# Attention in 64x64 quadrants with all steps placed anew, and MoE2 rows split one by one at unit 0

## The chip, the cores and the metric

The kernel runs on one core of one Trainium2 chip. The metric is the device time in microseconds of one execution; it is the median of the timed runs. A profile is one more execution, taken with the hardware profiler, and it has a time of its own.

## What is computed

Three stages follow one another on 4608 tokens of 512 numbers, all f32.

```python
kv  = einsum('bhsd,bhse->bhde', k, v)         # 8 batches, 8 heads, 576 tokens, 64 wide
out = einsum('bhsd,bhde->bhse', q, kv)
x   = out / sqrt(mean(out*out, -1) + 1e-6) * g_norm     # rows of 8 heads x 64
# MoE 1: 8 experts, the two best of noisy logits, 512 -> 1024 -> 512
nl  = x @ w_gate + log1p(exp(x @ w_noise)) * noise
x   = sum over the two: weight * relu(x @ w1[e]) @ w2[e]
# MoE 2: only rows with x @ w_skip > 0, the best of 8 experts, result added to x
x   = x + gate * relu(x @ w21[e]) @ w22[e]
```

## The kernel before

**Attention** (lines 300 to 870) runs over four pairs of batches. A batch is loaded as 128 partitions x 4 tokens (512 tokens, `load_kv`, `load_q`), and the remaining 64 tokens of two batches together as 128 partitions (`load_rest`). `kv_half` (L414, L419) sums k-transposed times v of four heads: 128x128 matmuls of two tokens each, of which the diagonal 64x64 blocks are wanted. Two copies and an addition (L422, L424, L313) bring the sums into a block-diagonal tile `kvbd` of 160 columns per head: 2 x 64 of kv and 2 x 16 of the router's gate columns, which `gate_columns` makes from kv (L440 to L449). The output runs in 56 steps (`subs`), 14 for each pair: transpose q of two or three heads on TensorE (`q_transposed`, L461) two steps ahead, copy (L464 or L466), multiply with `kvbd` (`out_sub`, L479; L485 and L486 for the remaining tokens), copy out (L488 or L490), square (L493 or L495), sum (L499). `finish` then makes the inverse root mean square of up to 16 values a row (L515 to L519, and a Newton step in `log_recip_newton`, L144 to L146), scales the rows on GpSimd (L523), sums the logits (L544, L547) and splits the rows into two f16 halves (L527 on ScalarE, L530 on VectorE), which SP writes to `xrows` in DRAM (L705, L709).

The order of all this is written by hand. Each step has three slots, and `at(step, f, slot)` puts a call there; the constants at the head of the file say where (`KV`, `GC`, `FIN`, `ROUTE`, `WSTEPS`, `EPLAN`, `CLEAR`) and which engine copies or squares (`QTE`, `OSBE`, `SQE`). All engines and SP's DMA queue run in the order of the program.

**Routing** (`route_half`) ranks the tokens of four batches in 27 pieces; the first half is placed by `ROUTE` beside the steps of the later pairs, the second runs in the **tail**: `TAIL` lists the order of its pieces ("r"), of what is left of `finish` ("f") and of the pieces of four early tiles of expert 0 ("0" to "3", `early_tile`, L734 to L753). Then the loop over the experts of MoE 1 begins with a gather of rows and a transposing DMA (L1055, L1057).

**MoE 2** works in units of one or two tiles of 128 rows of one expert (`moe2_unit`). `layer1` makes four pieces (for two tiles) and calls `point(p)` after each; ScalarE and VectorE make the two f16 halves of the hidden rows (L238, L239); `layer2` follows (L269). The rows of the next units are gathered in `later`, squared (`row_scales`, L931) at point 1 and split (`split_parts`, L938, L939) at point 3, in both cases all rows of a unit at once, and transposed by SP (L1194). The weights of a later unit are gathered behind the last tile of a unit (`rank_weights`, L1147), 2 MB each for `wa` and `wb`.

## Time and profile before

| | us |
|---|---|
| timed runs | 1273.98, 1275.65, 1279.09 |
| median | 1275.65 |
| profiled execution | 1287.97 |
| its span, first to last instruction | 1285.8 |

Busy shares of the profiled span: TensorE 92%, VectorE 64%, ScalarE 52%, GpSimd 29%. Times in the rows are counted from the span's start. A busy TensorE is not TensorE at its peak, since its ends are modelled; the pitch from start to start tells the price of a matmul in a row of them. "issue" is time in which an engine waited for nothing that the profile shows.

### The profile page before, as it was taken

To read this page: it belongs to the slowest core of one execution; us is meant where nothing else is said; L and a number is where in the kernel's file an instruction comes from. 1 tells how busy PE (TensorE), PEld (TensorE's weight loads), DVE (VectorE), ACT (ScalarE), POOL (GpSimd) and SP (SyncE) were. 2 spreads that over 40 slices of the span, in tenths; PEclk is the share of its full clock that TensorE was granted. 3 is DMA by queue.
4 is the path that set the end of the run, shared out by engine and by line. 5 is a ranking of instruction groups with operands and counts; after the bars stand their busy time and mean duration, and the time that the engine had idled before them with its cause. 6 is when DMAs were issued, how large, how long until landed. Compare 5 with 4: busy or idle time off the path is not lost.

```text
span 1285.8 us, 25287 instructions
## 1 busy us (share of the span) xinstructions
PE 1187.7 (92%) x9341; PEld 843.1 (66%) x9341; DVE 822.6 (64%) x3014; ACT 663.4 (52%) x1209; POOL 372.7 (29%) x454
## 2 busy tenths in 40 slices
PE   5868779999999999999999999999899999899996
PEld 5767667666666666676767576676666666576664
DVE  1667887535686777687677878778877665232231
ACT  2578663156564765675666767557664331132110
POOL 2223242211323232323333233232332331312220
PEclk8979789999999999999999999999999999999998
DMA  9999984748996978699698899989995673866570
GB/s 238 277 248 298 320 222 102 183 141 265 276 239 173 242 252 230 189 241 291 145 301 275 240 326 253 282 226 252 317 291 179 165 206 114 255 218 209 181 246 16
DMA packets 311410, 293.33 MB, mean 228 GB/s; under 512 B 205023, under 2 KB 256223, under 8 KB 307181
## 3 DMA queue, kind: packets, MB, share of 16 engines
q1 hardware_dynamic: 288316, 208.22, 61.8%
q0 software_dynamic: 22384, 82.36, 18.4%
q8 instruction: 75, 1.23, 0.4%
q10 hardware_dynamic: 576, 1.05, 0.2%
q14 instruction: 59, 0.48, 0.1%
HBM read 172.86 MB, written 93.42 MB: 207 GB/s over the span
## 4 chain that ended last, share of the span: by engine, by line
PE 52%; issue 15%; DVE 13%; ACT 11%; POOL 3%; another core or an unknown queue 2%; SPq 2%; DMA 1%; POOLq 0%; DVEq 0%; ACTq 0%
PE b L269 24%; PE a L230 21%; ACT wa L188 2%; PE kvps L414 1%; ACT hh L238 1%; DVE xh L939 1%; DVE x L1113 1%; ACT wb L188 1%; POOL out_dram L1211 1%; PE b L479 1%; PE small L968 1%; ACT ysb L1109 1%; DVE hl L239 1%; ACT presplit L188 1%
## 5 line engine op out<-in xcount | busy, mean ns | idle before, releaser
L230 PEld LDWEIGHTS <-wa 128*128 128x128 f16 x5184 | 460.0, 99 | 68.3 <-issue 21.3
L230 PE MATMUL a<-xT,wa 128*128 128x256 f16 (+6 forms) x3648 | 389.9, 267 | 8.3 <-issue 5.5
L269 PE MATMUL b<-wb,hh 128*128 128x512 f16 x1488 | 339.8, 379 | 8.7 <-ACT hh L238 8.5
L269 PEld LDWEIGHTS <-hh 128*128 128x128 f16 x1488 | 140.2, 98 | 170.8 <-ACT hh L238 19.5
L238 ACT ACTIVATE hh<-a 128x512 f16<-128x512 f32 (+5 forms) x186 | 107.1, 578 | 223.0 <-PE a L230 187.1
L239 DVE SCALAR_TENSOR_TENSOR hl<-a,hh 128x512 f16<-128x512 f32 (+5 forms) x186 | 125.1, 675 | 99.8 <-ACT hh L238 91.6
L269 PE MATMUL b<-wb,hl 128*128 128x512 f16 x744 | 175.8, 379 | 0.0
L1055 POOL DMA_INDIRECT xg<-xrows,idxp x67 | 65.6, 979 | 327.4 <-DVE orow L1079 287.0
L269 PEld LDWEIGHTS <-hl 128*128 128x128 f16 x744 | 72.2, 98 | 88.4 <-DVE hl L239 3.0
L230 PE MATMUL a<-x2Tr,wa 128*128 128x256 f16 (+1 forms) x1152 | 110.2, 258 | 8.1 <-DMA x2Tr<-xh 7.6
L1109 ACT ACTIVATE ysb<-b,gate 128x512 f32<-128x512 f32 x73 | 49.8, 682 | 128.3 <-PE b L269 68.8
L1117 POOL DMA_INDIRECT out_dram<-x,oi x67 | 68.3, 1020 | 137.2 <-DVE pi L1025 62.9
L171 ACT ACTIVATE wjunk<-stage 128x1024 bf16<-128x1024 f32 x96 | 101.3, 1055 | 2.1
L189 DVE SCALAR_TENSOR_TENSOR presplit<-stage,wscl,presplit 128x1024 f16<-128x1024 f32 x64 | 80.5, 1279 | 16.1 <-ACT presplit L188 16.1
L1088 POOL DMA_INDIRECT yo<-ydram,gi x67 | 70.9, 1059 | 51.1 <-issue 17.7
L188 ACT ACTIVATE presplit<-stage,wscl 128x1024 f16<-128x1024 f32 x64 | 71.3, 1141 | 17.9 <-DVE wscl L181 16.5
L479 PE MATMUL b<-kvbd,qTs 128*128 128x160 f32 x256 | 52.8, 346 | 21.9 <-issue 10.0
L931 ACT ACTIVATE jk<-x 128x512 bf16<-128x512 f32 x67 | 42.3, 631 | 54.6 <-DVE x L1113 48.3
L938 ACT ACTIVATE xh<-x,x2ss 128x512 f16<-128x512 f32 x67 | 45.4, 715 | 33.1 <-DVE x2ss L137 29.9
L523 POOL TENSOR_TENSOR osb<-osb,rinv 128x1024 f32<-128x1024 f32 (+1 forms) x20 | 37.1, 1854 | 87.0 <-DVE rinv L146 71.3
L479 PEld LDWEIGHTS b<-kvbd,qTs 128*128 128x128 f32 x256 | 42.6, 219 | 26.6 <-issue 10.9
L1113 DVE TENSOR_TENSOR x<-ysb,yo 128x512 f32<-128x512 f32 x67 | 46.4, 692 | 18.5 <-ACT ysb L1109 14.7
(356 smaller groups left out, 1529.8 us busy)
## 6 DMA issues: line engine op xcount, KB each, us to landing
stage<-in_moe_w_dram SPq DMA_DIRECT2D x32, 2048.0 KB
wsd<-presplit SPq DMA_DIRECT2D x8, 2056.0 KB
ydram<-ysb SPq DMA_DIRECT2D x64, 256.0 KB
wsd<-presplit SPq DMA_DIRECT2D x8, 2048.0 KB
out_dram<-zeros SPq DMA_DIRECT2D x9, 1024.0 KB
km<-in_k_dram SPq DMA_DIRECT2D x16, 512.0 KB
vm<-in_v_dram SPq DMA_DIRECT2D x16, 512.0 KB
qm<-in_q_dram SPq DMA_DIRECT2D x16, 512.0 KB
```

What stands on the lines that cost most here:

```text
L171: A.activation(junk, st[:, F * c:F * c + F], AF.Square, accum_out=acc[:, c:c + 1], **kw)
L188: A.activation(hi[:, d], st[:, d], AF.Copy, scale=sc)
L189: V.scalar_tensor_tensor(lo[:, d], st[:, d], sc, hi[:, d], op0=ALU.mult, op1=ALU.subtract)
L230: PE.matmul(ps[:, i, :], a[:, c, fs], xT[:, b + c, 0:nt], start=(n == 0), stop=(n == 11))
L238: behind[0] = A.activation(hh[:, fsl, 0:nt], ps, AF.Relu).ins
L239: i = V.scalar_tensor_tensor(hl[:, fsl, 0:nt], ps, 0.0, hh[:, fsl, 0:nt], op0=ALU.max, op1=ALU.subtract)
L269: PE.matmul(ps, a[:, f, gsl], b[:, f, :], start=(fs.start == 0 and i == 0), stop=(fs.stop == 8 and a is hl and f == 7))
L479: PE.matmul(po[:, i, :], qT[:, i, :], kvb[b % 4][:, h0 + i, :], start=True, stop=True)
L1055: G.indirect_dma_start(out=xg[:, g], out_offset=None, in_=xrows, in_offset=bass.IndirectOffsetOnAxis(ap=idx[:, t0 + g:t0 + g + 1], axis=0))
L1088: G.indirect_dma_start(out=yo, out_offset=None, in_=ydram[0:BASE[e], :], in_offset=bass.IndirectOffsetOnAxis(ap=gi[:, g:g + 1], axis=0), b ...
L1109: A.activation(ysb, ps, AF.Copy, scale=gate[:, g:g + 1])
L1117: s = G.indirect_dma_start(out=out, out_offset=bass.IndirectOffsetOnAxis(ap=oi[:, g:g + 1], axis=0), in_=x2[:, g], in_offset=None, bounds_ ...
```

## The change

**Loads.** q, k and v of four heads of a batch are loaded as 64 partitions x 9 tokens, the even heads on the lower 64 partitions and the odd heads on the upper ones; nine tokens of a head are one piece of 2304 bytes. There is no rest to load. Noise and router columns (`aux`) follow the same layout.

**Products.** kv of a pair of batches is summed in 64x64 quadrants: the row half `c` is the parity of the head, the column half `bl` the batch of the pair. `kv_out` copies the sums into `kvb` (two tiles in place of four, 80 columns per head and batch, no zeros) and GpSimd copies each half onto the other partitions. The output has 40 steps, ten for each pair: four heads of both batches at a time, two tokens after one another (one at the last), again in quadrants. q is transposed one step ahead instead of two.

**Norms.** One chain of Ln, Exp and three VectorE operations serves two pieces of two tokens. Rows are scaled on GpSimd as before; 15 of 20 low halves are subtracted on GpSimd (`LOX`), 24 of 40 squares are made there (`SQE`, 5 before), and all eight one-hot products of routing (`RHE`, four before).

**Places.** All places are new: weights of expert 0 start in step -5, the nine clears of the output stand in steps 19 to 38, routing and early tiles too; of early tile 0 four of eight pieces stand ahead of the tail instead of six. PSUM holds two "a" tiles in attention instead of three, and three behind it.

**MoE 2.** At unit 0 the rows of the next unit are squared and split one by one at points 0 to 2; a unit with one tile has its squares behind the last tile of the unit before, and its follower is split at point 1.

```diff
+KVAT = (-6, -5, -4, -4)
...
+CLEAR = (28, 19, 31, 21, 23, 28, 31, 38, 23)
...
+NT, NP = 9, 4
+ZT = 0
+FINS = ((2, 1), (2, 1))
+FINA = ((2, 2), (2, 1), (4, 0), (4, 1), (4, 2))
+FINB = ((2, 2), (2, 2), (5, 1), (6, 0), (7, 1))
...
+QTE = 'AVAAAVVAAAVAVVAAAVVVAAAVVAAVAAVAAVVAAAAV'
+OSBE = ('AA', 'AV', 'AV', 'VA', 'VA', 'AA', 'AV', 'AA', 'AV', 'AA', 'AA', 'VA', 'VA', 'AA', 'AA', 'AA', 'AA', 'VA', 'VA', 'VV', 'AA', 'VV', 'AA', 'AA', 'AA', 'AA', 'AA', 'AA', 'AA', 'AA', 'AA', 'AA', 'AA', 'AA', 'AA', 'AA', 'AV', 'AA', 'AV', 'AA')
+SQE = 'AGGAGAGGGGGGAAGAGAGGGGGAGAGAGGGGAAAAGGAA'
+KVE = 'AAVV'
+GTE = 'AVAV'
+LOE = "VVVVVVVV"
+RHE = 'GGGGGGGG'
+LOX = 'VGGVVGGGGGGGGGGVGGGV'
...
+QLEAD = 1
+KVOUT, GATE1, GATE2 = ((4, 1), (2, 1), (1, 2))
+SSAT = (1, 2)
+OSBB, X16B = 4, 3
+QLOAD = (-6, -3, 7, 17)
+
+WSTEPS = ((-5, 0, 2, 3, 4, 5, 9, 9, 9, 10), (10, 15, 16, 17, 19, 20, 20, 31, 31, 31))
...
+EPLAN = (((35, 0), (36, 0), (39, 1), (40, 0)), ((35, 0), (40, 1)), (), ())
...
+TAIL = '0 0 f f r 0 r 0 r r r 1 2 f r 2 1 r f r 1 1 r r r 1 r r 1 3 3 2 f r f r 2 r r r 3 3 2 r 2 r r 3 r r r 3 3 r r 3 r 2 2'
...
+        def load(nm, src, pb, hh, bufs):
+            t = ld.tile([P, 2, 2, NT, DH], F32, name=nm + "m", bufs=bufs)
             for bl in range(2):
+                SP.dma_start(t[:, bl].rearrange("p h r d -> p h (r d)"),
+                             src[2 * pb + bl, 4 * hh:4 * hh + 4].rearrange("(h c) (p r) d -> (c p) h (r d)", c=2, r=NT))
+            QT[nm, pb, hh] = t
+
+        def load_kv(pb, hh):
+            load("k", k, pb, hh, 2)
+            load("v", v, pb, hh, 2)
+
+        def load_q(pb, hh):
+            load("q", q, pb, hh, 3)
+
+        load_kv(0, 0)
+        load_kv(0, 1)
+        load_q(0, 0)
...
+        def kv_part(pb, hp):
+            km, vm = QT["k", pb, hp // 2], QT["v", pb, hp // 2]
+            o = hp % 2
+            if hp == 0:
+                kvps[pb] = [psum["kv"].tile([P, 4, DH], F32, name="kvps") for _ in range(2)]
+            for r in range(NT):
+                for bl in range(2):
+                    for c in range(2):
+                        sc, sb = slice(64 * c, 64 * c + 64), slice(64 * bl, 64 * bl + 64)
+                        PE.matmul(kvps[pb][c][sb, hp, :], km[sc, bl, o, r, :], vm[sc, bl, o, r, :],
+                                  start=(hp == 0 and r == 0), stop=(hp == 3 and r == NT - 1), skip_group_check=True)
+
+        def kv_out(pb):
+            kv = kvb[pb % 2]
+            for c, ps in enumerate(kvps.pop(pb)):
+                for bl in range(2):
+                    sb, so = slice(64 * bl, 64 * bl + 64), slice(64 - 64 * bl, 128 - 64 * bl)
+                    if KVE[2 * c + bl] == "A":
+                        A.activation(kv[sb, c::2, bl, 0:DH], ps[sb], AF.Copy)
+                    else:
+                        V.tensor_copy(kv[sb, c::2, bl, 0:DH], ps[sb])
+                    G.tensor_copy(kv[so, c::2, bl, 0:DH], kv[sb, c::2, bl, 0:DH])
...
+        def gate_columns(pb):
+
+            kv = kvb[pb % 2]
+            kvT = []
             for bl in range(2):
+                tp = psum["kv"].tile([64, H, DH], F32, name="kvps")
+                for h in range(H):
+                    PE.transpose(tp[:, h, :], kv[0:64, h, bl, 0:DH], ident[0:64, 0:64])
+                kvT.append(wk.tile([64, H, DH], F32, name="kvT", bufs=2))
+                if GTE[bl] == "A":
+                    A.activation(kvT[bl], tp, AF.Copy)
+                else:
+                    V.tensor_copy(kvT[bl], tp)
+            yield
+            for bl in range(2):
+                gp = psum["kv"].tile([P, H, 16], F32, name="kvps")
+                for h in range(H):
+                    for c in range(2):
+                        PE.matmul(gp[64 * c:64 * c + 64, h, :], kvT[bl][:, h, :], gw[:, h, :], start=True, stop=True)
+                if GTE[2 + bl] == "A":
+                    A.activation(kv[:, :, bl, DH:DH + 16], gp, AF.Copy)
+                else:
+                    V.tensor_copy(kv[:, :, bl, DH:DH + 16], gp)
...
+        def q_transposed(i):
+
+            pb, m, hh = subs[i]
+            r = min(2 * m, NT - 2)
+            tp = psum["a"].tile([P, 4, P], F32, name="a")
+            for j in range(4):
+                PE.transpose(tp[:, j, :], QT["q", pb, hh][:, j // 2, j % 2, r:r + 2, :], ident)
+            qT = wk.tile([P, 4, P], F32, name="qTs", bufs=QLEAD + 1)
...
+        def out_sub(i, qT, osb):
+            pb, m, hh = subs[i]
+            kv = kvb[pb % 2]
+            cs = range(2) if 2 * m + 1 < NT else (1,)
+            po = {c: psum["b"].tile([P, 4, DH + 16], F32, name="b") for c in cs}
+            for j in range(4):
+                for c in cs:
+                    for bl in range(2):
+                        sc, sb = slice(64 * c, 64 * c + 64), slice(64 * bl, 64 * bl + 64)
+                        PE.matmul(po[c][sb, j, :], qT[sc, 2 * bl + j // 2, 64 * (j % 2):64 * (j % 2) + 64], kv[sc, 4 * hh + j, bl, :],
+                                  start=True, stop=True)
             hs = slice(4 * hh, 4 * hh + 4)
+            for t, c in enumerate(cs):
+                if OSBE[i][t] == "A":
+                    A.activation(osb[:, t, hs], po[c], AF.Copy)
                 else:
+                    V.tensor_copy(osb[:, t, hs], po[c])
+            n = len(cs)
+            sq = wk.tile([P, 2, 4, DH], F32, name="sq", bufs=2)[:, 0:n]
+            x = osb[:, 0:n, hs, 0:DH]
+            if SQE[i] == "A":
+                A.activation(sq, x, AF.Square)
             else:
+                G.tensor_tensor(sq, x, x, op=ALU.mult)
+            return sq
...
+        def finish(i, group, ss):
+
+            N = sum(n for _, n, _, _ in group)
+            rinv = rt.tile([P, 4, H], F32, name="rinv", bufs=2)[:, 0:N]
+
+            def roots():
+                A.activation(rinv, ss[:, 0:N], AF.Ln, scale=1.0 / 64.0, bias=eps)
                 A.activation(rinv, rinv, AF.Exp, scale=-0.5)
 
+            def newton():
+                t = rt.tile([P, 4, H], F32, name="rmsa", bufs=1)[:, 0:N]
+                V.scalar_tensor_tensor(t, rinv, -1.0 / 64.0, rinv, op0=ALU.mult, op1=ALU.mult)
+                V.scalar_tensor_tensor(t, ss[:, 0:N], 64.0e-6, t, op0=ALU.add, op1=ALU.mult)
+                V.scalar_tensor_tensor(rinv, t, 3.0, rinv, op0=ALU.add, op1=ALU.mult)
+
+            steps = list(zip(FINS, (roots, newton)))
+            for p, (m, n, osb, L) in enumerate(group):
+                steps += finish_rows(i, m, n, osb, L, rinv[:, 2 * p:2 * p + n], p)
+            for (d, slot), f in sorted(steps, key=lambda x: x[0]):
+                if i + d < len(subs) + 1:
+                    at(i + d, f, slot=slot)
                 else:
...
+        def finish_rows(i, m, n, osb, L, rinv, p):
+
+            pb = subs[i][0]
+            xv, zv = osb[:, 0:n, :, 0:DH], osb[:, 0:n, :, DH:DH + 16]
+            x16 = []
+
+            def scale():
+                G.tensor_tensor(xv, xv, bc(rinv[:, :, :, None], [P, n, H, DH]), op=ALU.mult)
+
+            def gate_products():
+                (G if ZT else V).tensor_tensor(zv, zv, bc(rinv[:, :, :, None], [P, n, H, 16]), op=ALU.mult)
+                V.tensor_reduce(L, zv.rearrange("p t h n -> p t n h"), axis=AX.X, op=ALU.add)
+
+            def part(c):
+                return x16[0][:, 0:n, c:c + D].rearrange("p t (h d) -> p t h d", d=DH)
+
+            def high():
+                x16.append(wk.tile([P, 2, 2 * D], F16, name="x16", bufs=X16B))
+                A.activation(part(0), xv, AF.Copy)
+
+            def low():
+                (G if LOX[5 * pb + m] == "G" else V).tensor_tensor(part(D), xv, part(0), op=ALU.subtract)
+
+            def rows_out():
+                t0 = 1 + NT * P * pb
+                SP.dma_start(xrows[t0:t0 + NT * P, 0:512].rearrange("(p r) w -> p r w", r=NT)[:, 2 * m:2 * m + n],
+                             x16[0][:, 0:n].rearrange("p t w -> p (t w)").bitcast(F32).rearrange("p (t w) -> p t w", w=512))
+
+            sums_done[0] = gate_products
+            return list(zip(FINB if p else FINA, (scale, gate_products, high, low, rows_out)))
...
+                (G if RHE[4 * half + 2 * a + u] == "G" else V).tensor_tensor(rhs, bc(ohv[:, a, js, :, None], [P, 9, 8, T1]),
...
+        subs = [(pb, m, hh) for pb in range(NP) for m in range(5) for hh in range(2)]
+        FIRST = -8
+        for pb in range(NP):
+            s0 = 10 * pb
+            for hp in range(4):
+                step = s0 + KVAT[hp]
+                at(step, kv_part, pb, hp)
+                if hp % 2 and pb + 1 < NP:
+                    at(step + 1, load_kv, pb + 1, hp // 2, slot=0)
+            if pb == 0:
+                at(QLOAD[0], load_q, 0, 1, slot=0)
+                at(QLOAD[1], load_q, 1, 0, slot=0)
+            if pb + 1 < NP:
+                at(s0 + QLOAD[2], load_q, pb + 1, 1, slot=0)
+            if pb + 2 < NP:
+                at(s0 + QLOAD[3], load_q, pb + 2, 0, slot=0)
+            g = gate_columns(pb)
+            at(s0 - KVOUT[0], kv_out, pb, slot=KVOUT[1])
+            for d, slot in (GATE1, GATE2):
+                at(s0 - d, next, g, None, slot=slot)
+        at(FIRST, gate_weights)
         W0 = []
+        for g, steps in zip(first_weights(0, w1, w2, gcol, 0.5, W0, True), WSTEPS):
...
+            else:
+                if u >= 0 and k == len(units[u][1]) and u + 1 < len(units) and len(units[u + 1][1]) == 1:
+                    squares(u + 1)
+                if stream:
+                    stream.pop(0).gather(osc2)
...
+        def squares(self, n=2):
+
+            xs = [xg[:, 0] for xg in self.xg[self.ready:][:n]]
             if xs and not self.scales:
                 self.scales = (xs, row_scales(xs))
 
-        def split(self):
-
-            self.squares()
+        def split(self, all_rows=True):
+
+            if all_rows:
+                self.squares()
...
+    def between(u):
+
+        one = len(units[u][1]) == 1
+
+        def point(p):
+            if u == 0 and p < 3:
+                split(u, False)
+                if p < 2:
+                    R2[1].squares(1)
+            elif p == 1:
+                split(u, False) if one else squares(u)
+            elif p == 3:
+                split(u)
+        return point
+
     for u in range(len(units)):
-        moe2_unit(units[u][0], R2[u], later(u), lambda p, u=u: squares(u) if p == 1 else split(u) if p == 3 else None)
+        moe2_unit(units[u][0], R2[u], later(u), between(u))
```

## Rows read from the trace of the kernel before

**Rows 1.** First line of the page: span and instructions.
```profile
span 1285.8 us, 25287 instructions
```

**Rows 2.** Stretches: length, busy us (count) PE PEld DVE ACT POOL, clock, DMA, GB/s.
```profile
28.74:199.86 171.12, 133.97 (x1020) 121.90 (x1021) 126.66 (x310) 116.51 (x260) 53.53 (x43) 0.86 0.95 267
199.86:241.47 41.61, 39.56 (x445) 27.91 (x443) 30.35 (x88) 10.74 (x23) 14.37 (x24) 1.00 0.45 109
```

**Rows 3.** Waits of PE in 28.74:199.86: total us, times, longest us.
```profile
PE b L479 <- issue: 10.0, 3, 3.8
...
PE b L479 <- POOL kvbd L313: 6.6, 2, 4.2
```

**Rows 4.** Time line of PE: start us, us, engine, line, operation [idle before].
```profile
29.99 0.98 PE L479 MATMUL b<-kvbd,qTs 128*128 128x160 f32 x6
...
30.81 0.49 PE L461 MATMUL a<-ident,qm 128*128 128x128 f32 x3
...
31.13 1.95 PE L414 MATMUL kvps<-vm,km 128*128 128x128 f32 x16
...
33.01 0.71 PE L419 MATMUL kvps<-vl,kl 64*128 64x128 f32 x4
...
58.38 0.55 PE L461 MATMUL a<-ident,qm 128*128 128x128 f32 x3
58.85 0.45 PE L485 MATMUL b<-kvbd,qTs 128*64 128x128 f32 x4
...
59.66 0.55 PE L461 MATMUL a<-ident,qm 128*128 128x128 f32 x3
...
151.26 0.70 PE L485 MATMUL b<-kvbd,qTs 128*64 128x128 f32 x4
...
152.71 0.90 PE L461 MATMUL a<-ident,qm 128*128 128x128 f32 x3
...
228.79 0.87 PE L669 MATMUL small<-rhs,ohp 128*128 128x80 f16 x18
229.50 5.53 PE L230 MATMUL a<-xTe,wa 128*128 128x128 f16 x96
```

**Rows 5.** Groups by shape in 0:220: busy us, mean ns, idle before.
```profile
L523 POOL TENSOR_TENSOR osb<-osb,rinv 128x1024 f32<-128x1024 f32 x16 | 32.8, 2048 | 72.3 <-DVE rinv L146 62.9 <-DVE zt L544 9.4
...
L530 DVE TENSOR_TENSOR x<-osb,x 128x1024 f16<-128x1024 f32 x16 | 19.6, 1224 | 10.1 <-ACT x L527 10.0
```

**Rows 6.** Time line of PE at the end of the tail.
```profile
199.65 0.28 PE L486 MATMUL b<-kvbd,qTs 128*64 128x32 f32 x4
...
240.04 0.17 PE L862 MATMUL small<-cum,ones 128*128 128x8 f16 x1
...
241.47 10.64 PE L230 MATMUL a<-xT,wa 128*128 128x256 f16 x96 [1.04 <-DMA xT<-xg]
```

**Rows 7.** Time lines of DVE and POOL around the first one-hots.
```profile
159.78 2.36 DVE L660 TENSOR_TENSOR ohp<-iop,ph 128x1152 f16<-128x1152 f16 x1
...
165.99 1.35 DVE L660 TENSOR_TENSOR ohp<-iop,ph 128x1152 f16<-128x1152 f16 x1
...
159.54 5.42 POOL L663 TENSOR_TENSOR rhs<-ohv,oht 128x720 f16<-128x720 f16 x3 [0.84 <-DVE ohv L653]
```

**Rows 8.** Stretches of 5 us, columns as in rows 2.
```profile
5.00:10.00 5.00, 1.73 (x8) 1.76 (x9) 0.00 (x0) 0.00 (x0) 3.48 (x4) 1.00 1.21 279
...
1105.00:1110.00 5.00, 5.00 (x25) 2.23 (x23) 2.49 (x7) 1.45 (x3) 0.00 (x0) 1.00 0.99 412
```

**Rows 9.** MoE2 units: time line of PE; then issues of the x2Tr transposes.
```profile
1120.27 13.28 PE L230 MATMUL a<-x2Tr,wa 128*128 128x256 f16 x96 [5.32 <-DMA x2Tr<-xh]
...
1143.74 10.64 PE L230 MATMUL a<-x2Tr,wa 128*128 128x256 f16 x96
...
1177.37 10.64 PE L230 MATMUL a<-x2Tr,wa 128*128 128x256 f16 x96 [1.12 <-DMA x2Tr<-xh]
...
L1194 SPq DMA_TRANSPOSE x2Tr<-xh x2: 1346/4150/6954, 1106.7 to 1108.1; - x2
```

More of the change, by code (lines that the diff above doesn't have):

```diff
@@ L435, in gate_columns @@
-        def gate_columns(b):
-            bd = kvb[b % 4]
-            tp = pSm[0].tile([P, 4, DH], F32, name="small")
-            for hp in range(4):
-                PE.transpose(tp[:, hp, :], QT["kv", b, hp // 2][:, hp % 2 * 2:hp % 2 * 2 + 2, :], ident[0:64, 0:64])
-            kvT = wk.tile([P, 4, 2, DH], F32, name="kvT", bufs=1)
-            A.activation(kvT, bc(tp[:, :, None, :], [P, 4, 2, DH]), AF.Copy)
-            yield
-            gp = pSm[0].tile([P, 4, 2, 16], F32, name="small")
-            for hp in range(4):
-                PE.matmul(gp[:, hp], kvT[:, hp], gbd[:, hp, :], start=True, stop=True)
-            for c in range(2):
-                sl = slice(64 * c, 64 * c + 64)
-                A.activation(bd[sl, :, 128 + 16 * c:144 + 16 * c], gp[sl].rearrange("p a b n -> p (a b) n"), AF.Copy)
@@ L1196, in split @@
             self.ready += len(xs)
-            if self.ready < len(self.xg):
+            if all_rows and self.ready < len(self.xg):
                 self.split()
```

335 lines of the change are left out of this document (80 added, 255 removed).

## The prediction

> **What bounds the kernel now.** I read the views in this order: the page's span and busy shares, the busy times stage by stage, who waited for whom on TensorE, TensorE's time line, the durations by shape on the other engines, and the time line of the last 190 us.
>
> The profiled execution spans 1285.8 us [rows 1]. The change touches two of its stretches. The first is attention: its first output matmul starts at 28.74 us, its last one at about 199.86 us, and the expert loop starts at 241.47 us. In the 171.12 us of output steps no engine is full: TensorE 133.97, VectorE 126.66, ScalarE 116.51, GpSimd 53.53 us, granted clock 0.86, DMA share 0.95 [rows 2]. So the stretch is bound by the order of the steps on the in-order engines, with VectorE at 126.66/171.12 = 0.74 of the time, and TensorE waits at the seams between batches: 10.0 us in three waits without a visible releaser, 6.6 us in two for GpSimd's copy into the block-diagonal tile [rows 3]. Behind it, from 199.86 to 241.47, TensorE is busy 39.56 of 41.61 us at clock 1.00 [rows 2], with the early expert tiles: that tail is bound by TensorE, and the routing chain ends in it only 1.04 us later [rows 6]. A gain in the attention steps therefore moves the tail forward, and does not shorten it.
>
> The second stretch is the change-over from unit 0 to unit 1 of MoE2. TensorE waits 5.32 us there for the transposed rows, and the unit behind the wait takes 13.28 us where the next one of the same size takes 10.64 [rows 9]. So one late transfer costs 5.32 + 2.64 = 7.96 us.
>
> **Part 1, TensorE's work in attention.** Warm prices, from start to start [rows 4]: an f32 pass of 128x128 by 128 columns (31.13 to 33.01, 16 of them) 117 ns; by 160 columns (29.99 to 30.81, 6) 137 ns; an f32 transpose (30.81 to 31.13, 3) 107 ns. Each f32 matmul is two passes. Before, with the counts of the code, the output steps cost about 208 x 0.117 + 52 x 0.16 + 256 x 0.137 + 136 x 0.107 = 82 us, and some 23 us for the narrow passes, gate columns, routing and one early tile: 105 us of warm work in 171.
>
> After, the products use 64x64 quadrants: per pair of batches 144 kv matmuls, 144 output matmuls and 32 gate matmuls, two passes each, so 640 passes, and 2560 in all. The first pair's kv and gates lie before the first output, so 2208 lie in the output steps, beside 160 + 48 transposes and the routing and early-tile passes (about 26 us). A quadrant pass is not in this trace. Its bounds: 39 ns, the pitch of f16 passes of 80 columns (18 from 228.79 to 229.50), the nearest sign of how fast small passes are issued; 51 ns, the pitch of 16 passes that use half the array's columns (58.85 to 59.66); 91 ns, the same 16 at the low clock (151.26 to 152.71) [rows 4]. By columns alone (107 ns for 128, so 27 for 32) those 16 would take 8 x 107 + 8 x 27 = 1070 ns in line, and they took 810: halves of the array already overlap. I take 39 ns, because quadrants can overlap in two directions and the kv loop changes the row half with every matmul: 2208 x 0.039 + 26 = 112 us. The step from whole-array transposes to half-array passes took 0.47 instead of 0.32 us (58.38 to 58.85), 0.15 us each [rows 4]; at 45 such steps that is up to 6 us more, so 118. At 51 ns the sum is 145, at 91 ns 233; at 27 ns (64 columns are half of 107, two passes side by side), 92.
>
> The Trainium skill, "TensorEngine Tiling (Array Packing)", Key Properties, says that tiles load weights and multiply independently, but that a change of tiling mode drains the array. By the first half the low figure would hold and the sum be nearer 92; the second half speaks against this change, which alternates whole-array transposes with quadrants in every step. The trace agrees with a small drain, the 0.15 us above; no row shows loads of two row halves side by side.
>
> **Part 2, the other engines in the output steps.** VectorE: 15 of the 20 low-half subtractions go to GpSimd (13 x 1.22 and 2 of half size [rows 5]: -17 us); 20 norm chains of four small operations become 12 of three (-7); the additions that join two kv halves go (-7); copies of kv, gates and wider transposes come (+8); 126.7 - 23 = 104. ScalarE loses most squares and the kv moves, about 30 us: some 87. GpSimd: 53.5 + 28 for the subtractions (15 at the 2.05 us that its 128x1024 product takes [rows 5]) + 19 for 24 squares = 101. A GpSimd subtraction that writes f16 is not in the trace; its ends are VectorE's 1.22 and GpSimd's 2.05, and what it does to VectorE is open: VectorE's one-hot took 2.36 us beside GpSimd's f16 product and 1.35 beside f32 work [rows 7]. All eight of those products are now GpSimd's, so up to 4 more one-hots are stretched by 1 us.
>
> Nobody falls below about 100 us, and VectorE stays the fullest of the three. At the present 0.74 its 104 us need 141 us; TensorE's 118 at a clock of 0.86 need 137 plus seams of about 10. I take 147 us for the steps.
>
> **Part 3, loads and start.** q, k and v come in rows of 2304 bytes instead of 256, 512 and 1024. At the start such small rows ran at 279 GB/s with the share at 1.21, while the 16 KB weight rows of MoE2 ran at 412 at 0.99 [rows 8]. All that moves in the stage, some 52 MB, needs 52/0.35 = 149 us between those ends: no bound if the queue isn't held up. On SP's queue the nine 1 MB clears move earlier with the steps, and loads of the next pair stand behind row writes that wait for a subtraction that GpSimd now makes; a load has some six steps of slack before its kv step, about 20 us, so I count nothing, and one seam of 4 us a pair where that cover fails. But a pair of batches must now be loaded whole: 4.7 MB at 0.29 land at about 2 + 16 = 18 us, then 144 quadrant passes (6 to 13 us), copies and gates (about 6): first output at about 34 us, 5 later than now. Last output: 34 + 147 = 181, against 199.86.
>
> **Part 4, the tail.** The early tile 0 has two steps fewer done when the tail begins: 48 matmuls of 128 columns, 2.8 us more for TensorE; the cover that hides routing stays. Its layer-1 pieces share two PSUM tiles instead of three; a piece takes TensorE 2.8 us, which is longer than the two reads of the piece before, so no wait is counted. The expert loop starts at about 181 + 41.6 + 2.8 = 225.4: 16 us earlier. If GpSimd's products make routing the last to end, that costs up to 4 us.
>
> **Part 5, MoE2.** The transposes for unit 1 were issued at 1106.7 and 1108.1 us and the second issue took 6.95 us [rows 9], in the middle of two weight gathers. Row by row the first can be ready about 4 us earlier and the second 3, because squares and split no longer wait for both rows and for the fourth quarter of layer 1. The new wait is ScalarE's: its squares wait for the first gather with the outputs of layer 1 queued behind them, then VectorE's low halves, then TensorE's next tile; three PSUM tiles cover that for one quarter, 2.7 us. I take 3 of 5.32 us and half of the 2.64 of low clock: 4.4. The units with one tile lose two waits of about 1.1 us ([rows 9] has one of the two); I count 1.6. Together 6 us; ends 0 (the transfers stay behind the weights) and 10.
>
> **The sum** is 16 + 6 = 22 us. It is made against the profiled span of 1285.8; the timed runs lie at 1273.98 to 1279.09 with median 1275.65, 10 us below, and I carry the difference over: 1275.65 - 22 = 1254.
>
> **Rivals.** A, forecast: 39 ns and balanced engines, 1254. Chance 0.45.
> B, quadrant passes stay at 51 ns because weight loads go one after another: TensorE has 145 us, at a clock of about 0.92 and 10 us of seams 168; last output at 202, loop 5 us later, MoE2 gives 6: 1275, between 1264 and 1279. For it: the half-array passes stand at just 51 ns. Against it: they shared all rows. Chance 0.24.
> C, other side: the low clock stays through the quadrant passes, so that they cost 75 ns as a mean of both levels. 2208 x 0.075 + 32 = 198 us, steps of about 205, loop 41 us later, less 6: 1310. It decides from about 54 ns a pass. For it: the same passes took 91 ns at granted clock 0.50 after idle time [rows 4]. Against it: passes lie closer together than before. Chance 0.15.
> D, weight loads and passes of different quadrants run side by side throughout: 27 ns, 92 us of TensorE work, no seam that waits for it, steps in which VectorE's 104 us are 0.82 of the time, 127 us. The loop starts 35 us earlier, with 6 from MoE2 that is 1235. For it: the two halves that overlap already; against it: TensorE is not the only bound. Chance 0.12. The Trainium skill's independent tiles (same page and section) would be this case.
> E, the MoE2 edit does not do what it says (0 us) while A holds: 1260. Chance 0.04.
>
> About 0.5% (6.4 us) is what a measurement can tell from no change. Faster: A, D, E and a third of B, 0.69. Same: 0.13 of B. Slower: C and the rest of B, 0.18. For 8 in 10 the range goes from D, 1235, over A and B to the near side of C, 1284.
>
> **What would show it.** In the changed profile: the pitch of quadrant passes (39, 51 or more), the output steps' length (147) with VectorE near 104 and GpSimd near 101 us, the first output at 34 us, the loop's start at 225, and the wait ahead of MoE2 unit 1 (2 instead of 5.32). The forecast is wrong if the pitch is over 54 ns, or if GpSimd's f16 work holds VectorE up so that it needs over 120 us.

## The result

The changed kernel is slower: 1287.06 us, the median of 10 runs (1278.52 to 1295.43), where the kernel before has 1277.88 in 10 runs beside it; ratio 1.0077 [1.0049, 1.0105]. On another chip it was 1.0052 [1.0017, 1.0087] (experiment 1). The forecast was 1254, with 1235 to 1284 as its range.

The page of the changed kernel begins:

```profile
span 1280.0 us, 28791 instructions
```

Its stretches (columns as in [rows 2]): the output steps from first to last output matmul, the tail, and three parts of the steps:

```profile
30.58:196.10 165.52, 114.16 (x2518) 95.47 (x2518) 135.15 (x230) 85.75 (x175) 101.64 (x74) 0.69 0.76 248
196.10:246.93 50.83, 44.41 (x493) 31.01 (x492) 32.94 (x80) 12.14 (x25) 27.57 (x30) 0.97 0.46 117
...
60.00:80.00 20.00, 10.45 (x192) 8.35 (x186) 19.61 (x27) 10.03 (x18) 14.34 (x9) 0.60 0.75 255
80.00:100.00 20.00, 15.29 (x485) 12.94 (x484) 12.27 (x21) 13.49 (x30) 9.91 (x9) 0.84 0.90 330
...
160.00:180.00 20.00, 8.01 (x115) 6.52 (x119) 19.73 (x24) 8.30 (x15) 13.19 (x8) 0.50 0.48 141
```

Against [rows 1, 2, 6] the first output comes 1.8 us later, the steps take 5.6 us less (165.5 for 171.1), the tail 9.2 us more (50.8 for 41.6): the expert loop starts at 246.93 for 241.47, 5.5 us later. From the first MoE2 unit to the end it is 231.7 us for 234.9. Together that is +2.3 us. MoE1, which the change does not touch, took 801.4 us in this execution and 809.4 in the one profiled before; a kernel with the old attention took 799.1 (experiment 6). Over all profiles of this study the stage scatters from 794 to 819 us, so those 8 us are no gain of the change, and they hide the loss when the two spans are compared. Both profiled executions of the changed kernel (1281.72, and 1276.38 in experiment 1) are faster than the medians beside them; where its slower executions, 1285 to 1295 us, lose the rest was not profiled, and stays open.

In the two stretches with VectorE at 19.6 to 19.7 of 20 us TensorE is busy 10.45 and 8.01 us, and its granted clock is 0.60 and 0.50; 0.50 is the lower level, 1.2 GHz. Over all the steps TensorE stands idle 165.5 - 114.2 = 51 us. Who waits, on TensorE in 30.58:196.1:

```profile
PE small L644 <- DVE ohp L635: 15.4, 2, 11.4
PE b L453 <- DVE osb L460: 10.1, 3, 5.1
PE b L453 <- issue: 8.1, 4, 3.2
PE b L453 <- ACT osb L458: 5.8, 3, 5.1
```

The longest one, on the time lines of VectorE, GpSimd and TensorE; the first two are a piece of a weight split that begins before GpSimd's next operation, a square, and that square:

```profile
71.91 1.27 DVE L198 SCALAR_TENSOR_TENSOR wa<-stage,wscl,wa 128x1024 f16<-128x1024 f32 x1
...
72.13 1.95 POOL L467 TENSOR_TENSOR sq<-osb 128x512 f32<-128x512 f32 x1 [3.69 <-DVE ss L471]
...
162.15 1.35 DVE L484 SCALAR_TENSOR_TENSOR rmsa<-rinv 128x8 f32<-128x8 f32 x1
163.53 2.06 DVE L485 SCALAR_TENSOR_TENSOR rmsa<-ss,rmsa 128x8 f32<-128x8 f32 x1
165.62 0.96 DVE L486 SCALAR_TENSOR_TENSOR rinv<-rmsa,rinv 128x8 f32<-128x8 f32 x1
...
168.38 5.93 DVE L198 SCALAR_TENSOR_TENSOR wb<-stage,wscl,wb 128x1024 f16<-128x1024 f32 x3
...
163.44 2.13 POOL L518 TENSOR_TENSOR x<-osb,x 128x1024 f16<-128x1024 f32 x1
165.53 1.04 POOL L467 TENSOR_TENSOR sq<-osb 128x512 f32<-128x512 f32 x1
...
168.93 3.10 POOL L518 TENSOR_TENSOR x<-osb,x 128x1024 f16<-128x1024 f32 x1
...
175.70 0.78 PE L644 MATMUL small<-rhs,ohp 128*128 128x80 f16 x9 [11.42 <-DVE ohp L635]
```

L484 to L486 are the correction of the inverse root, three VectorE operations that here work on eight numbers a partition. The second starts 0.09 us after GpSimd's subtraction (L518) and ends 0.02 us after it; alone it takes 0.17. Three pieces of a split take 5.93 us for 3 x 1.27. The later one is stretched on GpSimd too: the square that begins inside the split takes 1.95 us for 1.04, the last subtraction 3.10 for 2.13. By these lines, an estimate, VectorE reaches the one-hots for which TensorE waits (L635) some 6 us late, of the 11.4. This is the theory the experiments had to test: **GpSimd's new work holds up VectorE's operations with two SBUF operands**. The Trainium skill, "SBUF — State Buffer", section "Who interferes with whom", has the rule: such an operation contends with a GpSimd instruction that reads SBUF, not with one that only writes it, and the second to start waits for the whole of the first. The trace agrees (2.06 us against 0.17), and the rule spoke against this change; the forecast did not weigh it.

Beside it stood two rivals. Rival 2: GpSimd's in-order queue is the late chain. Rival 3: the placing of the steps, or the quadrants, set the time, and the two engines don't matter.

### The profile page after: what moved, and what is told of

Its sections match the earlier page's. It is cut to its first block, busy times and chain, and to the rows that moved or that the text cites. A ratio compares the mean times of both kernels' runs of the same rounds, so it can differ in the third digit from the quotient of the medians.

```text
span 1280.0 us, 28791 instructions
## 1 busy us (share of the span) xinstructions
PE 1169.2 (91%) x11181; PEld 823.0 (64%) x11181; DVE 833.7 (65%) x2935; ACT 634.3 (50%) x1121; POOL 428.8 (33%) x482
## 5 line engine op out<-in xcount | busy, mean ns | idle before, releaser
L453 PE MATMUL b<-kvb,qTs 64*64 64x80 f32 x1152 | 48.8, 295 | 27.7 <-DVE osb L460 10.1
L453 PEld LDWEIGHTS b<-kvb,qTs 64*64 64x64 f32 x1152 | 39.1, 181 | 38.1 <-issue 16.6
L1192 POOL DMA_INDIRECT out_dram<-ysb,mrow x16 | 16.3, 1017 | 123.5 <-DVE ysb L1190 123.5
```

What stands on the lines that cost most here:

```text
L453: PE.matmul(po[c][sb, j, :], qT[sc, 2 * bl + j // 2, 64 * (j % 2):64 * (j % 2) + 64], kv[sc, 4 * hh + j, bl, :], start=True, stop=True)
```

## The experiments

A ratio is always to the kernel before on the same chip, with its 95% interval. Chips differ (the kernel before took 1275 to 1287 us), so ratios are compared, not microseconds. "Lows" are the subtractions that make the low halves of the rows. Stages, from one profile each, in us:

| kernel | ratio | steps | tail | loop starts |
|---|---|---|---|---|
| changed, again (1) | 1.0052 [1.0017, 1.0087] | 163.5 | 55.0 | 249.4 |
| lows on VectorE (2) | 0.998 [0.9963, 0.9997] | 164.4 | 48.4 | 243.6 |
| the same, other chip (2) | 0.999 [0.9962, 1.0018] | 163.3 | 48.6 | 242.3 |
| short zeros for lows (3) | 0.9912 [0.9887, 0.9938] | 158.5 | 48.7 | 237.8 |
| long zeros for lows (3) | 0.9961 [0.9932, 0.9989] | 154.3 | 48.6 | 233.6 |
| squares on ScalarE (4) | 1.0026 [1.0002, 1.0049] | 164.7 | 54.1 | 249.4 |
| GpSimd relieved (4) | 1.0016 [0.999, 1.0042] | 162.2 | 48.4 | 241.3 |
| correction on GpSimd (4) | 1.0056 [1.003, 1.0082] | 168.8 | 51.9 | 251.2 |
| that and lows on VectorE (4) | 1.0008 [0.9988, 1.0028] | 164.7 | 49.3 | 244.7 |
| old attention, lows on GpSimd (5) | 1.0069 [1.0043, 1.0094] | 177.4 | 47.4 | 254.6 |

### 1. The changed kernel again

> The changed kernel itself once more, beside the next three on one chip. All theories: 1285 to 1290; its profile says whether the 165 us of steps, the 51 us of tail and the 801 us of MoE1 (809 before) come back. If MoE1 gives 801 again and the next kernel but one, with the old attention, gives 801 too, the 8 us of MoE1 were scatter of the execution profiled before.

Measured 1.0052; MoE1 794.1 us. The steps came back within 2 us, the tail was 4 us longer than the first time because the transfers of the first rows ended later (TensorE waited 6.2 us for `xT`). So single profiles of the tail scatter by some 4 us.

### 2. The low halves back on VectorE

```diff
-LOX = 'VGGVVGGGGGGGGGGVGGGV'
+LOX = 'VVVVVVVVVVVVVVVVVVVV'
```

> The changed kernel with all 20 low-half subtractions on VectorE (13 of the 15 that GpSimd had lie in the output steps). Theory 1 (VectorE operations that read two SBUF operands wait out whole GpSimd operations, and this fills VectorE): VectorE gets some 16 us of subtractions and sheds about 27 of GpSimd's 97 us share of some 28 us of stretching, about 8 us; its busy time in the output steps goes from 135 to about 143 us, the steps from 165.5 to about 170, the run to about 1288 to 1292. Rival 2 (GpSimd's own 102 us of work in the steps is the late chain): GpSimd falls to about 73 us and the steps shrink by 10 us or more, about 1275. Rival 3 (quadrants and the placing of the steps set the time, not the two engines): no change, 1285 to 1289.

> The changed kernel with all lows on VectorE once more, as the base of the next three: a ratio to the kernel before of 0.998, as the first time, if it holds from chip to chip.

Measured 0.998 and 0.999: the loss is gone. VectorE's busy time is the same, 135.95 and 137.06 us for 135.15, so what it got (17 us of subtractions) it shed in stretching; the theory had expected to see only half of that, and a run of 1288. The loop starts 3.3 to 7.0 us earlier, nearly all of it in the tail. The time is the one that rival 2 named, but the steps did not shrink by its 10 us: they are as long with the subtractions on either engine.

### 3. Zeros in place of the subtractions, short and long

```diff
-(G if LOX[5 * pb + m] == "G" else V).tensor_tensor(part(D), xv, part(0), op=ALU.subtract)
+if LOX[5 * pb + m] == "G":
+    G.memset(part(D), 0.0)
```

The long zeros repeat the last line, and write 3 of the 8 heads a third time.

> The changed kernel in which GpSimd writes zeros in place of its 15 low-half subtractions (a part of the computation left out: the low halves of those rows are zero): GpSimd still writes the same bytes but reads nothing. Theory 1: VectorE's operations beside it keep their short times, VectorE's busy time in the output steps falls by 8 to 14 us, and so do the steps: run about 1273 to 1279. Rival 2 (GpSimd's work is the late chain): shorter only by as much as the zeros are quicker than the 2.07 us of a subtraction. Rival 3: no change, 1285 to 1289.

> The changed kernel in which GpSimd writes zeros twice (and a part a third time) in place of each of its 15 subtractions, some 2.1 us each, as long as the subtraction (again the low halves of those rows are left out): GpSimd is as long busy as in the changed kernel, but reads nothing in that time. If the loss comes from VectorE's operations being held up while GpSimd reads (lock), the ratio stays near the 0.991 of the short zeros, at most 0.995, and VectorE's root corrections keep a median of 0.19 us. If it comes from the time in GpSimd's queue, the ratio goes back to 1.005 and the output steps to 164 or 165 us.

Measured 0.9912 and 0.9961. The steps with the long zeros, then two of VectorE's corrections with their shortest, median and longest time in ns, over the steps and the start of the tail:

```profile
30.64:184.98 154.34, 106.91 (x2519) 89.41 (x2519) 123.04 (x230) 85.64 (x175) 105.93 (x99) 0.76 0.80 264
...
L484 DVE SCALAR_TENSOR_TENSOR rmsa<-rinv x12: 168/192/1348, 45.3 to 190.8; 128x32 f32<-128x32 f32 x8, 128x8 f32<-128x8 f32 x4
...
L485 DVE SCALAR_TENSOR_TENSOR rmsa<-ss,rmsa x12: 166/191/193, 45.5 to 191.0; 128x32 f32<-128x32 f32 x8, 128x8 f32<-128x8 f32 x4
```

and in the changed kernel:

```profile
L484 DVE SCALAR_TENSOR_TENSOR rmsa<-rinv x11: 184/587/2071, 45.2 to 193.1; 128x32 f32<-128x32 f32 x8, 128x8 f32<-128x8 f32 x3
...
L485 DVE SCALAR_TENSOR_TENSOR rmsa<-ss,rmsa x11: 166/192/2060, 45.4 to 193.3; 128x32 f32<-128x32 f32 x8, 128x8 f32<-128x8 f32 x3
```

GpSimd is busy 105.93 us, more than the 101.64 of the changed kernel, but reads nothing while it writes the zeros. VectorE's time falls from 135 to 123 us: some 12 us of it were waits beside the subtractions, and the corrections show where. The steps fall from 164 or 165 to 154 us and the ratio from 1.0052 and 1.0077 to 0.9961, about 1% of the run. So GpSimd's busy time is not what costs this 1%.

Whether the hold-up of VectorE alone costs it is not shown, because the zeros differ in a second way. A subtraction needs the f16 half that ScalarE makes first; until that is there, it stands at the head of GpSimd's queue, and what is behind it waits too. With the long zeros no such wait is left. GpSimd's waits for ScalarE's half, in the steps of the changed kernel, of the one with the squares on ScalarE (experiment 4) and of the old attention with lows on GpSimd (experiment 5):

```profile
POOL x L518 <- ACT x L515: 7.2, 3, 5.5
...
POOL x L518 <- ACT x L515: 37.1, 10, 6.7
...
POOL x L531 <- ACT x L527: 25.0, 12, 3.5
```

The second of these has VectorE at 124.89 us, hardly more than with the long zeros, and its steps still take 164.7. So VectorE's load does not set the steps alone. A kernel whose zeros wait for ScalarE was not run, and how the 10 us split between the two stays open. The short zeros give another 0.5% by the ratios, while their profiled steps were 4 us longer; what GpSimd's time in itself costs can't be told from them.

### 4. What else GpSimd does

```diff
-SQE = 'AGGAGAGGGGGGAAGAGAGGGGGAGAGAGGGGAAAAGGAA'
+SQE = 'AAAAAAAAAAAAAAAAAAAAAAAAAAAAAAAAAAAAAAAA'
```

That is the first; the relieved kernel also has the lows on VectorE and `RHE = 'GGGGVVVV'`.

> The changed kernel with all 40 squares on ScalarE (24 of them were GpSimd's, 25.6 us in the output steps). Theory 1: ScalarE goes from 86 to about 101 us, GpSimd from 102 to about 76, and VectorE loses about a quarter of its 28 us of stretching, 135 to about 128; steps 165.5 to about 158, run about 1279. Rival 2 (GpSimd's own work is the late chain): 10 us or more shorter, below 1277. Rival 3 (placing of steps, quadrants): no change or longer by what ScalarE gets, 1285 to 1295.

> The changed kernel with GpSimd's load as it was before the change: all lows on VectorE, all squares on ScalarE, the slot products of the second half on VectorE. Theory 1: VectorE 107 us of unstretched work + 16 of lows + about 6 of stretching = 129 against 135; steps about 160; the tail 4 us shorter because the last slot products take 0.9 instead of 2.1 us; run about 1277. Rival 2: about the same, 1270 to 1277. Rival 3 (quadrants, placing): the steps stay at 165, only the tail gains: about 1283.

Measured 1.0026 and 1.0016. The squares gave 0.3 to 0.5%, with intervals that overlap those of the changed kernel, and less than any expectation but the third: VectorE shed 10 us and the steps kept their 164.7. With GpSimd's load near the one before (48.77 us in the steps, for 53.53) VectorE has 129.03 us, as the theory said; the steps are still 162.2, and the kernel is level with the one before, no faster.

The correction moved off VectorE altogether (its 1e-6 is left out):

```diff
-V.scalar_tensor_tensor(t, rinv, -1.0 / 64.0, rinv, op0=ALU.mult, op1=ALU.mult)
-V.scalar_tensor_tensor(t, ss[:, 0:N], 64.0e-6, t, op0=ALU.add, op1=ALU.mult)
-V.scalar_tensor_tensor(rinv, t, 3.0, rinv, op0=ALU.add, op1=ALU.mult)
+G.tensor_tensor(t, rinv, rinv, op=ALU.mult)
+G.tensor_tensor(t, t, ss[:, 0:N], op=ALU.mult)
+G.tensor_scalar(t, t, -1.0 / 64.0, 3.0, op0=ALU.mult, op1=ALU.add)
+G.tensor_tensor(rinv, t, rinv, op=ALU.mult)
```

> The changed kernel with the correction of the norm's root (three tiny VectorE operations with two SBUF operands, each able to wait out a GpSimd operation) as four tiny operations on GpSimd itself, without its 1e-6: there it can wait for no lock, and the GpSimd product behind it follows in the same queue. Theory 1 (VectorE is filled by waiting for GpSimd): these operations took 17.3 us of VectorE in the output steps, 6 of them work; VectorE falls from 135 to about 120, steps by 8 to 12 us, tail by 2, run about 1272 to 1276. Rival 2 (GpSimd is the late chain): GpSimd gets some 10 us more, run 1285 or longer. Rival 3: no change.

> Both repairs: root correction on GpSimd, all lows on VectorE. Theory 1: VectorE 135.95 with the lows alone, less some 11 us of root corrections: 125; steps about 157 to 160, run about 1264 to 1268, faster than the kernel before by 0.6 to 0.9%. Rival 2 and 3: as with the lows alone, 1272 to 1275.

Measured 1.0056 and 1.0008: nothing gained, though VectorE fell to 118.18 us in the steps. The time line of the first shows where the wait went:

```profile
163.39 2.50 POOL L639 TENSOR_TENSOR rhs<-ohv,oht 128x720 f16<-128x720 f16 x1
...
165.85 2.13 POOL L519 TENSOR_TENSOR x<-osb,x 128x1024 f16<-128x1024 f32 x1
...
167.94 0.20 POOL L484 TENSOR_TENSOR rmsa<-rinv 128x8 f32<-128x8 f32 x1
...
169.03 1.11 DVE L508 TENSOR_TENSOR osb<-osb,rinv 128x128 f32<-128x128 f32 x1 [4.40 <-POOL rinv L487]
...
170.46 7.06 DVE L198 SCALAR_TENSOR_TENSOR wb<-stage,wscl,wb 128x1024 f16<-128x1024 f32 x3
...
178.92 0.78 PE L645 MATMUL small<-rhs,ohp 128*128 128x80 f16 x9 [12.49 <-DVE ohp L636]
```

The correction is ready at 163.4 and runs at 167.94, behind a product and a subtraction in GpSimd's queue; VectorE idles 4.40 us for it, and the split behind it is still stretched. The same wait stands in GpSimd's queue instead of on VectorE. The theory's sum, a shorter VectorE gives shorter steps, is wrong; here the chain through GpSimd's queue is what is late.

### 5. The old attention with the same subtractions on GpSimd

```diff
-V.tensor_tensor(lo, xv, hi, op=ALU.subtract)
+lows[0] += 1
+(G if 'VGGVVGGGGGGGGGGVGGGV'[lows[0] - 1] == "G" else V).tensor_tensor(lo, xv, hi, op=ALU.subtract)
```

> The kernel before with 15 of its 20 low-half subtractions on GpSimd, in the pattern of the changed kernel: the old attention, so no quadrants. Theory 1: the 15 take 2.07 us on GpSimd for 1.2 on VectorE, VectorE sheds 17 us of work and gains some 10 to 15 of stretching; steps stay within 4 us of 171, run 1272 to 1282; VectorE's tiny root operations show single times of 1 to 2 us in place of 0.17 to 0.20. Rival (only the crowded quadrant kernel suffers): the root operations keep 0.17 to 0.20 us, VectorE falls by 17 us, the run to about 1268.

Measured 1.0069, and its stretches, steps and tail:

```profile
29.85:207.20 177.35, 136.87 (x1021) 125.99 (x1022) 120.30 (x290) 116.28 (x260) 80.22 (x56) 0.82 0.92 255
207.20:254.58 47.38, 41.28 (x442) 28.09 (x443) 34.95 (x101) 10.72 (x23) 17.16 (x25) 0.96 0.46 105
```

This one edit costs the kernel before as much as the whole change does: steps 6 us longer, tail 6 us longer, with VectorE 6.4 us less busy than in [rows 2]. So the loss needs no quadrants and no new placing. Which of the two ways of experiment 3 it takes here, this run does not tell: GpSimd waits 25.0 us for ScalarE's halves, and VectorE's corrections show single times of up to 1.86 us, as the theory said, but keep a median of 0.17. Nor are two operands a condition: L515, a VectorE operation with one, was held up too (first the kernel before, then this one). It takes 0.17 us; the seven times of 0.97 to 0.98 us here all lie beside a GpSimd subtraction and end 0.03 us behind its end.

```profile
L515 DVE TENSOR_SCALAR vv<-ss x20: 171/174/418, 36.2 to 202.4; 128x16 f32<-128x16 f32 x16, 128x8 f32<-128x8 f32 x4
...
L515 DVE TENSOR_SCALAR vv<-ss x19: 171/207/982, 39.5 to 204.3; 128x16 f32<-128x16 f32 x16, 128x8 f32<-128x8 f32 x3
```

### 6. The edit of MoE2

> The changed kernel with its edit of MoE2 undone. If the edit gains what its stretch shows (3.2 us from the first MoE2 unit to the end), about 1290; if the longer wait ahead of unit 1 (7.3 for 5.3 us) makes it a loss, about 1284; if it does nothing, 1287.

> The kernel before with the edit of MoE2 alone. By the prediction's step of 6 us, a ratio of 0.995; by the traces' 3.2 us, 0.9975; by a rival (the edit does nothing, its gains are taken by the longer wait ahead of unit 1) 1.000. MoE1 in its profile: 801 us if the 809 before were scatter, 809 if the old attention causes them.

(`squares`, `split`, `later` and `between` of MoE2 taken back in the first, put into the kernel before in the second.) Measured 1.012 [1.007, 1.0169] without the edit, beside 1.0052 with it on the same chip, and 0.998 [0.9951, 1.0009] for the edit alone. From the first MoE2 unit to the end: 234.8 without, 231.3 with it; 229.8 in the old kernel with it, against 234.9. It gains 3.5 to 5 us in these pairs. Over all profiles the stretch takes 227.1 to 234.1 us with the edit (17 profiles) and 234.8 to 236.7 without it (3), so the gain stands clear of the scatter. In the changed kernel, and then in the one without the edit:

```profile
1119.01 12.15 PE L239 MATMUL a<-x2Tr,wa 128*128 128x256 f16 x96 [7.30 <-DMA x2Tr<-xh]
...
1172.74 10.64 PE L239 MATMUL a<-x2Tr,wa 128*128 128x256 f16 x96
```

```profile
1122.43 12.31 PE L239 MATMUL a<-x2Tr,wa 128*128 128x256 f16 x96 [8.16 <-DMA x2Tr<-xh]
...
1177.66 10.64 PE L239 MATMUL a<-x2Tr,wa 128*128 128x256 f16 x96 [1.07 <-DMA x2Tr<-xh]
1210.52 10.64 PE L239 MATMUL a<-x2Tr,wa 128*128 128x256 f16 x96 [1.17 <-DMA x2Tr<-xh]
```

The two single-tile waits, 2.2 us together, are gone; the wait ahead of unit 1 hardly moved: 7.30 and 7.76 with the edit for 8.16 without it, 5.36 for the 5.32 of [rows 9] in the old kernel. Where the rest of the gain lies was not followed.

### 7. The placing of the steps

Splits of expert 0's second weight at other steps, in the changed kernel; then splits one to a step on top of the lows on VectorE; then the slot products too:

```diff
-WSTEPS = ((-5, 0, 2, 3, 4, 5, 9, 9, 9, 10), (10, 15, 16, 17, 19, 20, 20, 31, 31, 31))
+WSTEPS = ((-5, 0, 2, 3, 4, 5, 9, 9, 9, 10), (10, 15, 16, 17, 19, 20, 20, 22, 24, 26))
+WSTEPS = ((-5, 0, 2, 3, 4, 5, 6, 7, 9, 10), (11, 15, 16, 17, 19, 20, 21, 22, 23, 24))
```

> The changed kernel with the last three pieces of expert 0's second weight split at steps 22, 24 and 26 in place of all three at step 31, ahead of the one-hots for which TensorE waited 11.4 us. If the placing causes that wait, it shrinks below 6 us, the steps by 5 us and the run to about 1280 (rival 3). By theory 1 VectorE is full in that stretch anyway, the wait moves to other matmuls, and the steps stay within 2 us: 1285.

> Lows on VectorE, and the eight splits of expert 0's weights one to a step (6, 7, 9, 10 and 21 to 24) in place of 9, 9, 9, 10 and 20, 31, 31, 31; the second load goes from step 10 to 11. If bursts of splits in VectorE's order hold the steps up, the long steps (10.2 us at step 14 and 12.9 at step 34 with the lows alone) fall by 3 us each or more, the output steps from 164 to about 156, ratio about 0.991. If the norm chains' way over GpSimd's squares and products sets these steps, within 2 us: 0.998.

> Lows on VectorE, splits spread one to a step, and the second half's slot products on VectorE. The last of these gave nothing by itself; if the tail's chain is now short enough for it, 3 us: ratio 0.993 to 0.994; if not, 0.996 as with the splits alone.

Measured 1.0056 [1.0027, 1.0084], 0.9962 [0.9939, 0.9986] and 0.9989 [0.9958, 1.002]. In the first the longest wait fell from 11.4 to 5.9 us and the steps stayed at 165.8: the wait moved to other matmuls, as the theory said. With the lows on VectorE, spreading gave 0.3% against its base, within the intervals of the two. Counted from transpose to transpose, step 34 fell from 12.9 to 9.4 us and step 14 from 10.2 to 7.5, but steps 11, 12 and 29 took back most of it (161.3 us for 163.3 in all). By this one measurement it is the best kernel of the study that computes everything, 0.4% faster than the one before (0.1 to 0.6%); the third, with the same splits, adds nothing that shows, and its interval holds 1.

### 8. The tail

Slot products of the second half on VectorE in the changed kernel; the last row group's norm chain put ahead of what is left of the rows before, on top of the lows on VectorE; and that with spread splits and products:

```diff
-RHE = 'GGGGGGGG'
+RHE = 'GGGGVVVV'
```

```diff
+elif i == len(subs) - 1 and f in (roots, newton, sums_done[0]):
+    first.append(f)
...
+late[:0] = first
```

> The changed kernel with the slot products of the second half back on VectorE, as in the kernel before. By the theory that the routing chain now ends the tail, each of four products goes from 2.1 us on GpSimd to 0.9 on VectorE and the one-hots beside them lose their 1 us: tail 51 down to about 46, run 1282. By the rival that the tail is longer because early tiles and their matmuls come later (48 more matmuls, lower clock), the tail stays at 50 to 51 and the run at 1287.

> Lows on VectorE, and in the tail the last row group's root, correction and gate products ahead of the two activations and subtractions of the rows before. If that order sets the longer tail, the slot indices come 3 us earlier after the last output (38 to 35 us), tail 48.4 to about 45, ratio about 0.9955. If the tail is bound by TensorE's early tiles, unchanged at 48: 0.998.

> Lows on VectorE, splits spread, last chain first, and the second half's slot products on VectorE. By the sum of the three: steps 156, tail about 44, ratio 0.987 to 0.990. If none of them is the cause, 0.998.

Measured 1.0087 [1.0052, 1.0122], 1.0161 [1.0122, 1.02] and 1.0084 [1.0056, 1.0113]. The products are not the cause: the tail was 52.6 us. The second order was a mistake of its own: with the gate products popped first, the tail's list no longer emits the rest of the rows ahead of routing, so two row writes left SP's queue only at 235.74, where with the lows alone the last one had left at 212.56, behind everything the gather waits for, and the tail grew to 63.7 us (63.2 in the third). It tells nothing of the norm chain. The tail of the changed kernel, on VectorE, GpSimd and TensorE:

```profile
202.75 2.05 DVE L485 SCALAR_TENSOR_TENSOR rmsa<-ss,rmsa 128x8 f32<-128x8 f32 x1
...
205.36 0.37 DVE L508 TENSOR_REDUCE L<-osb 128x16 f32<-128x128 f32 x1
...
235.97 1.00 POOL L1035 DMA_INDIRECT xg<-xrows,idx  x1 [3.87 <-DVE idx L669]
...
246.93 10.64 PE L239 MATMUL a<-xT,wa 128*128 128x256 f16 x96 [0.34 <-DMA xT<-xg]
```

The last logits are ready 9.6 us after the last output (before: 4.5), 2 of them a correction held up by a subtraction; the gather starts at 39.9 (before: 31.9), and the loop 11.0 us later (before: 9.7). With the 15 subtractions on GpSimd the tail of the new attention took 50.8 to 55.6 us in seven profiles, without them 48.2 to 49.3 in eight (the two with the other order aside): this is where the loss against the lows on VectorE shows. Of the 7 us that are left against 41.6, 4.4 are work of TensorE (busy 44.0 for 39.56), the rest is idle time, with 4.0 us of waits for the routing's one-hots; what lies behind both was not found.

## Why the prediction was wrong, point by point

**The bound** was named rightly, the order of the steps on in-order engines, and then not used: the sum divided TensorE's work by a clock (137) and VectorE's by a utilisation (141), took the longer of the two with 10 us of seams on TensorE's side, 147, and counted no other wait.

**Part 1, TensorE**, the term that decided between the rivals, was too high. Kv passes of 64 columns and output passes of 80, at the full clock (granted 1.00):

```profile
36.67 0.85 PE L453 MATMUL b<-kvb,qTs 64*64 64x80 f32 x32
37.45 0.66 PE L436 MATMUL a<-ident,qm 128*128 128x128 f32 x4
38.03 1.28 PE L392 MATMUL kvps<-vm,km 64*64 64x64 f32 x72
39.13 0.37 PE L453 MATMUL b<-kvb,qTs 64*64 64x80 f32 x9
```

(39.13 - 38.03)/72 = 15 ns and (37.45 - 36.67)/32 = 24 ns, where 39 was taken and 27 was the lower end. So the condition of rival D held and more, and its time did not follow: TensorE stood idle 51 us of the 165, not 10, and was busy the other 114 at a mean granted clock of 0.69. The change made the engine cheap that did not set the time.

**Part 2 is the step that failed**: it let the steps shrink with the busy times, 147 us with 10 of waits, and they took 165 with 51. "At the present 0.74 its 104 us need 141" is wrong at both ends. VectorE had 135 us, not 104; that it "needs over 120 us" was the prediction's own sign of being wrong, and it came. Of the 31 us, some 21 are the stretching of these groups of the output steps (busy us and mean ns behind the bar):

```profile
L507 DVE TENSOR_TENSOR osb<-osb,rinv 128x256 f32<-128x256 f32 (+1 forms) x19 | 13.4, 706 | 0.4
...
L484 DVE SCALAR_TENSOR_TENSOR rmsa<-rinv 128x32 f32<-128x32 f32 (+1 forms) x11 | 8.3, 752 | 5.8 <-ACT rinv L480 5.7
L198 DVE SCALAR_TENSOR_TENSOR wa<-stage,wscl,wa 128x1024 f16<-128x1024 f32 x4 | 7.4, 1892 | 0.0
L198 DVE SCALAR_TENSOR_TENSOR wb<-stage,wscl,wb 128x1024 f16<-128x1024 f32 x4 | 7.2, 1841 | 1.2 <-ACT wb L197 1.2
...
L485 DVE SCALAR_TENSOR_TENSOR rmsa<-ss,rmsa 128x32 f32<-128x32 f32 (+1 forms) x11 | 5.8, 526 | 0.4
...
L486 DVE SCALAR_TENSOR_TENSOR rinv<-rmsa,rinv 128x32 f32<-128x32 f32 (+1 forms) x11 | 3.2, 289 | 0.4
```

Alone the three corrections take 0.19 us, 33 x 0.19 = 6.3 of 17.3; the splits 8 x 1.27 = 10.2 of 14.6; the gate products at 0.42 (0.29 for the three of half size) 7.6 of 13.4. Without them VectorE would have 114; the other 10 us were not broken down. The long zeros took back 12 of VectorE's time, most of it in the corrections; the gate products stayed as long (14.9 us in 19), so GpSimd's other operations hold VectorE up as well. The row that showed it was cited, [rows 7], and misread: the one-hots at 1.35 us, from 165.99, were not "beside f32 work". GpSimd had ended its product at 164.96 and did nothing until

```profile
170.39 1.06 POOL L523 TENSOR_TENSOR osb<-osb,rinv 128x512 f32<-128x512 f32 x1 [5.43 <-DVE rinv L146]
```

So the row compared a GpSimd that reads with one that is idle, and was priced at "up to 4 more one-hots" instead of every operation of VectorE that can be held up; the text left open what the subtractions do to VectorE, and gave that no chance among the rivals. GpSimd's sum was right (101 for 101.6), ScalarE's too (87 for 85.8, against the text's own "Nobody falls below about 100 us"). And the utilisation was no lever: with VectorE at 118 us (correction on GpSimd) the steps took 169, with it at 137 (lows on VectorE) 163. What holds the steps at 162 us with GpSimd relieved, 15 above the forecast, was not found; the lows on GpSimd explain why the change lost, not why it did not gain 22 us.

**Part 3.** The first output came at 30.58, not 34; the loads were no bound, as forecast (share 0.76).

**Part 4.** The loop was to start 16 us earlier and started 5.5 later. The tail was forecast at 44.4; routing became the last to end, as the text allowed for "up to 4 us", but the tail took 50.8 and 55.0, which is 6 to 11 more than forecast, and GpSimd's products were not the cause (52.6 without them).

**Part 5.** 6 us forecast, 3.5 to 5 measured. The size was nearly right and the place wrong: the single-tile waits gave 2.2 us for 1.6, and the wait ahead of unit 1, from which 4.4 were to come, hardly shrank.

**The rivals.** B's time, 1275, is what the change comes to with GpSimd relieved, but not for B's reason. C was the slower case and its mechanism, dear passes at the low clock, did not happen: the low clock stood in the stretches in which TensorE was busy 8 to 10 of 20 us. The slower case that came true had been left out.

## What to carry to other kernels

Before work is moved from VectorE to GpSimd, list the VectorE operations that will run beside it, those with two SBUF operands first: in these runs each could wait for a whole GpSimd operation, whatever its own size, so that a chain of tiny ones can cost as much as the work that was moved. Ask too what the moved work itself waits for, and what then stands behind it in GpSimd's queue. An engine that is bound by the order of its steps is not costed by busy time over utilisation: find the waits that set the long steps, and ask of each part of a change whether it shortens one of those.
